# Column norms summed over partitions on GpSimd instead of by fp32 matmuls, and the library that this needs

## The chip, the cores and the metric

One core of a Trainium2 chip. The time is that of one whole execution in device microseconds (us). It differs from run to run by some tenths of a per cent, so medians of several runs are given. Kernels are compared with runs of the kernel before on the same chip. A ratio is the mean time of one kernel's fast runs over that of the other's fast runs of the same rounds, so it is not quite the ratio of the medians quoted beside it. A profile's span is some 1.8 us shorter than the time of its run.

PE is TensorE, ACT is ScalarE, DVE is VectorE and POOL is GpSimd. GpSimd also issues all loads of q, k, v and the weights.

## The reference, cut to what matters

```python
def _attn_ref(q, k, v, tau):                  # q, k, v: 4 x 5824 x 256, fp32
    qn = q / (np.linalg.norm(q, axis=1, keepdims=True) + 1e-06)
    kn = k / (np.linalg.norm(k, axis=1, keepdims=True) + 1e-06)
    s = kn.transpose(0, 2, 1) @ qn / tau      # 256 x 256 for each batch
    ...                                       # softmax of s over its last axis -> a
    return (v @ a).astype(np.float32)

def _moe_ref(x, w1, w2, w3, w_out):           # x: the result above, 23296 x 256
    a = x @ w1
    b = x @ w2
    h = a * b @ w3
    return (h @ w_out).astype(np.float32)
```

The norms run over the 5824 tokens. Tokens lie on partitions, so a norm needs a sum over partitions.

## The kernel before

The softmax matrix of a batch is folded into w1 and w2 ("Wf"), and w3 into w_out. The bulk of the work is then two wide products a and b for each chunk of v, their product on DVE, and one product o. While batch b goes through this, the scores of batch b+1 are accumulated (G), and the squares of its q and k are summed over time into one 128 x 2 x 256 tile. After the last score come the steps that I call the **tail** of batch b: sum over partitions, inverse norms, scaling, exponentials, row sums, folding. The steps are placed by a list of times on a clock of the kernel's own, near microseconds:

```python
def norms():
    a1 = work.tile([P, 2, C], F32, tag="acc1", ...)
    nc.vector.tensor_add(a1, accs[n][:, 0], accs[n][:, 1])
    st["ksq"] = a1[:, 1, :]
    st["qsq"] = a1[:, 0, :]
def k_row():
    m = psum.tile([P, 512], F32, tag="ab", ...)
    nc.tensor.matmul(m[:, :C], lhsT=ones_pp, rhs=st["ksq"], start=True, stop=True)   # fp32
    ...   # four activations: Ln, Exp, Ln, Exp
def q_sums():
    m = psum.tile([P, 512], F32, tag="ab", ...)
    for ct in range(CT):
        nc.tensor.matmul(m[:, ct:ct + 1], lhsT=st["qsq"][...], rhs=ones_f, ...)      # fp32
    q_norm(m[:, :CT])   # two activations, two small DVE instructions
...
# in the list of times: norms, k_row, q_sums, scaled (scaling and exponentials), sums, eight folds
ts = [t1 + 1.0, t1 + 3.5, t1 + 4.0, t1 + 8.0, t1 + 12.0] + [t1 + 13.0 + 0.9 * i for i in range(8)]
```

At the start GpSimd issues loads and, after the first two pieces, builds an identity matrix:

```python
load_piece("k", 0, 0, (half,))
load_piece("q", 0, 0, (half,))
masks.make_identity(nc, ident)      # on GpSimd: a memset and an affine select
nc.vector.tensor_copy(ident_b, ident)
...
for pi in range(1, 4):
    load_piece("k", 0, pi)
    load_piece("q", 0, pi)
```

## Time and profile before

| what | before |
|---|---|
| median of 4 runs | 575.73 us (575.41 to 576.57) |
| span of the profile; PE busy in it | 573.6; 561.9 us |
| mean granted PE clock | 1.000 |
| fp32 matmuls in one tail, from PE's starts | 0.80 us |

To see where time goes I cut the span at the first 'a' matmul of each batch. PE's timeline of the kernel before (start, length, engine, line, operation, count):

```profile
40.15 0.59 PE L425 MATMUL a<-vT,Wf 128*128 128x512 bf16 x2
...
183.03 0.59 PE L425 MATMUL a<-vT,Wf 128*128 128x512 bf16 x2
...
316.73 0.59 PE L425 MATMUL a<-vT,Wf 128*128 128x512 bf16 x2
...
450.10 0.59 PE L425 MATMUL a<-vT,Wf 128*128 128x512 bf16 x2
```

The differences are the stretches: start 40.15, batch 0 142.88, batch 1 133.70, batch 2 133.37 and batch 3 123.50 us. A tail lies in each of batches 0, 1 and 2.

### The profile page before, as it was taken

To read this page: it belongs to the slowest core of one execution; us is meant where nothing else is said; L and a number is where in the kernel's file an instruction comes from. 1 tells how busy PE (TensorE), PEld (TensorE's weight loads), DVE (VectorE), ACT (ScalarE), POOL (GpSimd) and SP (SyncE) were. 2 spreads that over 40 slices of the span, in tenths; PEclk is the share of its full clock that TensorE was granted. 3 is DMA by queue.
4 is the path that set the end of the run, shared out by engine and by line. 5 is a ranking of instruction groups with operands and counts; after the bars stand their busy time and mean duration, and the time that the engine had idled before them with its cause. 6 is when DMAs were issued, how large, how long until landed. Compare 5 with 4: busy or idle time off the path is not lost.

```text
span 573.6 us, 10125 instructions
## 1 busy us (share of the span) xinstructions
PE 561.9 (98%) x3760; PEld 357.0 (62%) x3766; DVE 374.1 (65%) x597; ACT 337.9 (59%) x624; POOL 71.0 (12%) x162
## 2 busy tenths in 40 slices
PE   8789999999999999999999999999999999999997
PEld 4755576776666666666666666666665666666665
DVE  0047744787967567887776567778876656565564
ACT  0046534777766567776765567767765555454453
POOL 5240020202010111221000012021100000000000
PEclk9999999999999999999999999999999999999999
DMA  8999959779574696495661596675740325221011
GB/s 163 211 194 208 188 99 235 175 171 213 134 185 108 123 207 151 95 190 120 147 147 49 117 192 143 132 142 119 184 110 38 85 74 146 63 63 74 38 71 59
DMA packets 74561, 76.93 MB, mean 134 GB/s; under 512 B 54161, under 2 KB 58257, under 8 KB 74513
## 3 DMA queue, kind: packets, MB, share of 16 engines
q0 software_dynamic: 15504, 39.46, 39.2%
q1 hardware_dynamic: 58784, 36.64, 21.1%
q8 instruction: 29, 0.48, 0.3%
q10 hardware_dynamic: 224, 0.20, 0.1%
q14 instruction: 20, 0.16, 0.1%
HBM read 78.91 MB, written 23.86 MB: 179 GB/s over the span
## 4 chain that ended last, share of the span: by engine, by line
PE 91%; DMA 5%; ACT 1%; issue 1%; DVE 1%; POOL 1%; ACTq 0%; POOLq 0%
PE o L466 27%; PE a L425 27%; PE b L425 27%; PE G L188 5%; DMA k<-in_k_dram 3%; PE fold L344 2%; DMA q<-in_q_dram 2%; PE w L575 1%; ACT as L431 1%; POOL k L109 0%; PE row L272 0%; POOL q L109 0%; DVE abs L440 0%; DVE osb L487 0%; ACT kr L276 0%
## 5 line engine op out<-in xcount | busy, mean ns | idle before, releaser
L440 DVE TENSOR_TENSOR abs<-as,b 128x512 bf16<-128x512 bf16 x336 | 229.7, 685 | 140.5 <-ACT as L431 128.7
L431 ACT CAST as<-a 128x512 bf16<-128x512 f32 (+1 forms) x384 | 215.4, 562 | 177.7 <-PE a L425 86.7
L425 PEld LDWEIGHTS <-Wf 128*128 128x128 bf16 x1536 | 149.1, 98 | 102.5 <-issue 2.6
L466 PE MATMUL o<-W_sb,abs 128*128 128x256 bf16 x1376 | 209.7, 273 | 0.5 <-ACT osb L486 0.4
L425 PE MATMUL a<-vT,Wf 128*128 128x512 bf16 x704 | 209.4, 379 | 0.4
L425 PE MATMUL b<-vT,Wf 128*128 128x512 bf16 x704 | 209.4, 379 | 0.0
L466 PEld LDWEIGHTS <-abs 128*128 128x128 bf16 x1376 | 134.5, 98 | 82.0 <-issue 0.6
L197 DVE TENSOR_TENSOR acc<-acc,sq 128x1024 f32<-128x1024 f32 x66 | 80.4, 1219 | 0.8 <-ACT sq L185 0.8
L188 PE MATMUL G<-k,q 128*128 128x256 bf16 x276 | 49.6, 273 | 0.0
L185 ACT ACTIVATE sq<-q 128x512 f32<-128x512 bf16 x66 | 41.8, 633 | 0.0
L185 ACT ACTIVATE sq<-k 128x512 f32<-128x512 bf16 x66 | 41.6, 630 | 0.0
L413 POOL COPY gate_t<-abs 1x1 bf16<-1x1 bf16 x39 | 12.1, 310 | 183.7 <-DVE abs L440 183.1
L487 DVE COPY osb<-o 128x512 f32<-128x512 f32 x44 | 30.1, 684 | 0.0
L188 PEld LDWEIGHTS <-q 128*128 128x128 bf16 x276 | 27.0, 98 | 3.1
L486 ACT COPY osb<-o 128x512 f32<-128x512 f32 x44 | 25.7, 585 | 4.6 <-PE o L466 2.6
L417 POOL COPY gate_t<-vT 1x1 bf16<-1x1 bf16 x17 | 4.0, 234 | 180.5 <-DMA vT<-v 145.1
L274 ACT ACTIVATE kr<-row 128x256 f32<-128x256 f32 x4 | 1.5, 384 | 34.0 <-PE row L272 34.0
L109 POOL DMA_DIRECT2D q<-in_q_dram x29 | 15.6, 538 | 12.5 <-DMA k<-in_k_dram 5.2
L344 PE MATMUL fold<-w,e 128*128 128x512 bf16 x61 | 16.5, 378 | 0.1
L351 ACT ACTIVATE Wf<-fold,rs 128x512 bf16<-128x512 f32 x16 | 10.9, 687 | 7.2 <-PE fold L344 4.3
L109 POOL DMA_DIRECT2D k<-in_k_dram x25 | 13.7, 550 | 3.9 <-DMA k<-in_k_dram 1.9
L109 POOL DMA_DIRECT2D v<-in_v_dram x25 | 13.4, 539 | 4.0 <-issue 2.6
(87 smaller groups left out, 219.1 us busy)
## 6 DMA issues: line engine op xcount, KB each, us to landing
out_dram<-osb SPq DMA_DIRECT2D x44, 512.0 KB, 3.1
k<-in_k_dram POOLq DMA_DIRECT2D x19, 512.0 KB, 8.8
v<-in_v_dram POOLq DMA_DIRECT2D x19, 512.0 KB, 5.1
q<-in_q_dram POOLq DMA_DIRECT2D x18, 512.0 KB, 6.5
w_wout<-in_moe_w_dram POOLq DMA_DIRECT2D x1, 2048.0 KB, 22.9
k<-in_k_dram POOLq DMA_DIRECT2D x4, 320.0 KB, 9.4
v<-in_v_dram POOLq DMA_DIRECT2D x4, 320.0 KB, 5.2
q<-in_q_dram POOLq DMA_DIRECT2D x4, 256.0 KB, 11.9
```

Source lines behind the costliest of these rows:

```text
L109: nc.gpsimd.dma_start(out=pieces[nm, n, pi][:, lo:hi, :], in_=qk_main[nm, n][0][:, pi * PIECE + lo : pi * PIECE + hi, :])
L185: nc.scalar.activation(out=dst[:, :, part, :], in_=src[:, o : o + 2, :], func=AF.Square)
L188: nc.tensor.matmul(G[:, ct, :], lhsT=qt[:, i, ct * P : (ct + 1) * P], rhs=kt[:, i, :], start=(pr == 0 and part == 0 and ct == 0), stop=(pr ...
L197: nc.vector.tensor_add(accs[n], accs[n], sqs[0])
L344: nc.tensor.matmul(st["fold", i], lhsT=st["e"][:, c2, c1 * P : (c1 + 1) * P], rhs=w12[:, c2, w, h * 512 : (h + 1) * 512], start=(c2 == 0), ...
L413: nc.gpsimd.tensor_copy(gate_t, last_ab[0][:1, :1])
L425: nc.tensor.matmul(t[:, :n], lhsT=Wf[b][:, ct, w, j * P : (j + 1) * P], rhs=rhs_of(b, c, ct), start=(ct == 0), stop=(ct == CT - 1),)
L431: nc.scalar.copy(a_sb[:, :n], tiles[0][:, :n])
L440: nc.vector.tensor_mul(ab, a_sb, tiles[1])
L466: nc.tensor.matmul(tl[h][:, o, :], lhsT=lhsT, rhs=W_sb[:, j, :], start=(j == 0 and o == 0), stop=(j == FT - 1 and (small or o == 1)), skip ...
L486: nc.scalar.copy(o[:, 0:2, :], tl[0])
L487: nc.vector.tensor_copy(o[:, 2:4, :], tl[1])
```

## The change

Its intent: take the fp32 matmuls from PE, the bound engine, and let idle GpSimd sum over partitions. The identity moves behind six pieces' load issues, so that a library load that GpSimd needs stands there. The tail's steps get new times, to leave room for the reduction. Cut to its core:

```diff
         def norms():
             nc.vector.tensor_add(a1, accs[n][:, 0], accs[n][:, 1])
-            st["ksq"] = a1[:, 1, :]
-            st["qsq"] = a1[:, 0, :]
+            tot = work.tile([P, 2, C], F32, tag="s", name=f"tot_{n}", bufs=1)
+            nc.gpsimd.partition_all_reduce(
+                tot.rearrange("p w c -> p (w c)"), a1.rearrange("p w c -> p (w c)"), P, ReduceOp.add
+            )
+            st["tot"] = tot
 ...  # k_row: the four activations read tot, no matmul, where n > 0
         def q_sums():
-            ...  # two fp32 matmuls
-            q_norm(m[:, :CT])
+            q_norm(diagonal(st["tot"][:, 0, :].rearrange("p (c t) -> p c t", t=P)))
 ...
-    masks.make_identity(nc, ident)
-    nc.vector.tensor_copy(ident_b, ident)
 ...
     for pi in range(1, 4):
+        if pi == 3:
+
+            masks.make_identity(nc, ident)
+            nc.vector.tensor_copy(ident_b, ident)
         load_piece("k", 0, pi)
 ...
-            t0, t1 = 58.0, 120.0
+            t0, t1 = 58.0, 118.0
 ...
-        ts = [t1 + 1.0, t1 + 3.5, t1 + 4.0, t1 + 8.0, t1 + 12.0] + [t1 + 13.0 + 0.9 * i for i in range(8)]
+        ts = [t1 + 1.0, t1 + 8.5, t1 + 9.0, t1 + 11.0, t1 + 14.5] + [t1 + 15.5 + 0.9 * i for i in range(8)]
```

"diagonal" multiplies two 128x128 blocks by the identity on DVE and sums each row, as batch 0 does before too.

## The prediction

> **What bounds the kernel now.** I read the page's busy table first, then the stretches of the span, then the three places where the removed matmuls stand, then the start. The busy table:
>
> ```profile
> PE 561.9 (98%) x3760; PEld 357.0 (62%) x3766; DVE 374.1 (65%) x597; ACT 337.9 (59%) x624; POOL 71.0 (12%) x162
> ```
>
> TensorE (PE) is busy for 561.9 of 573.6 us at full granted clock, so 11.7 us is all its idle time. GpSimd (POOL) has 88% of the span free. Taking matmuls from PE therefore shortens the span by about what they occupied, if nothing else makes PE wait. Their place in the first batch's tail, in PE's timeline (start, length, operation, count):
>
> ```profile
> 163.52 0.60 PE L466 MATMUL o<-W_sb,abs 128*128 128x256 bf16 x4
> 163.95 0.60 PE L272 MATMUL row<-acc,ones_pp 128*128 128x256 f32 x2
> 164.39 0.50 PE L283 MATMUL ss<-ones_f,acc 128*128 128x1 f32 x4
> 164.75 0.59 PE L425 MATMUL a<-vT,Wf 128*128 128x512 bf16 x2
> ...
> 167.71 0.38 PE L466 MATMUL o<-W_sb,abs 128*128 128x256 bf16 x2 [0.39 <-ACT osb L486]
> ```
>
> Lengths overlap because matmuls are pipelined; the cost is the distance between starts. The two fp32 groups hold PE from 163.95 to 164.75: 0.80 us. In the two later tails the same distance is 291.22 to 292.01 and 425.14 to 425.94, so 0.79 and 0.80 us. The last line is PE waiting 0.39 us for ScalarE (ACT), which the same norms had occupied:
>
> ```profile
> 163.29 0.58 ACT L431 CAST as<-a 128x512 bf16<-128x512 f32 x1 [0.71 <-PE a L425]
> 164.59 0.38 ACT L274 ACTIVATE kr<-row 128x256 f32<-128x256 f32 x1 [0.72 <-PE row L272]
> ...
> 166.50 0.21 ACT L292 ACTIVATE r<-r 128x2 f32<-128x2 f32 x1
> 166.61 0.56 ACT L431 CAST as<-a 128x512 bf16<-128x512 f32 x1
> ```
>
> Six activations hold ACT from 164.59 to 166.61, about 2.0 us, while every group of matmuls (1.30 us) leaves ACT only 0.7 us idle.
>
> The start is another regime: PE waits for loads. In the stretches (length, busy time by engine, clock, DMA share, GB/s) the transfers are saturated from 5 us on:
>
> ```profile
> 0.00:5.00 5.00, 3.75 (x9) 1.34 (x10) 0.91 (x7) 1.28 (x1) 3.89 (x12) 1.00 0.50 69
> 5.00:10.00 5.00, 5.00 (x40) 3.03 (x39) 0.00 (x0) 0.00 (x0) 3.28 (x7) 1.00 1.12 215
> 10.00:15.00 5.00, 4.06 (x55) 3.44 (x54) 0.17 (x1) 0.00 (x0) 1.05 (x2) 1.00 1.05 211
> 15.00:20.00 5.00, 2.97 (x36) 2.52 (x34) 0.00 (x0) 0.00 (x0) 0.56 (x1) 1.00 1.06 213
> ```
>
> GpSimd issues those loads. Its timeline shows that after eight issues (six pieces, the first two in halves) each further one waits until an earlier load has landed:
>
> ```profile
> 3.78 0.29 POOL masks.py:199 TENSOR_SCALAR_AFFINE_SELECT ident<-ident 128x128 f32<-128x128 f32 x1
> ...
> 5.60 0.57 POOL L109 DMA_DIRECT2D q<-in_q_dram  x1
> ...
> 8.06 0.53 POOL L109 DMA_DIRECT2D k<-in_k_dram  x1 [0.72 <-DMA q<-in_q_dram]
> 9.37 0.53 POOL L109 DMA_DIRECT2D q<-in_q_dram  x1 [0.78 <-DMA q<-in_q_dram]
> ```
>
> **What the Trainium skill says.** (1) "FP8 and Floating Point Precision", section TensorE Precision Notes: true fp32 is "4 passes through PE array". The trace agrees: the fp32 row of 256 columns holds PE for 0.44 us from start to start, as long as the four bf16 matmuls of 256 columns ahead of it (163.52 to 163.95, 0.43 us). (2) "GPSIMD Engine Reference", section 2.1: the first call to a freshly loaded kernel pays a load of approximately 6 us that shows as no instruction. The trace before can't show this: the identity's select begins within 0.1 us of the memset before it. (3) The same page, section 3: a two-input GpSimd operation runs at about 2.6 cycles an element at 1.2 GHz, and a partition-axis tensor_reduce of [128, 2048] takes 247,699 ns. No run here shows either. (4) "SBUF - State Buffer", section Who interferes with whom: a VectorE (DVE) instruction with at most one SBUF input outside the two-port modes doesn't contend with GpSimd. The tail's products read one operand from PSUM and last 0.69 us; I expect them unchanged beside the reduction.
>
> **The change part by part.**
>
> Removed: the row and the column sums of three tails. 0.80 + 0.79 + 0.80 = 2.39 us of PE on the path that sets the end. This is the certain gain: **-2.4 us**.
>
> Added on GpSimd: one all-reduce of 128x512 fp32 per tail. My estimate takes the page's 2.6 cycles: one pass over 512 elements is 512 x 2.6 / 1.2 GHz = 1.1 us, and folding partitions, passing sums along the cores and writing back is three to five such passes, so 3.3 to 5.5 us. In the tail after batch 0 the sum that feeds it is ready at 163.1 (DVE's 0.68 us from 162.40), and the schedule now puts the consumers 7.5 us of its own clock after the reduction, where it was 2.5. So it should be done before ACT asks. It also stays clear of the transfers: GpSimd issues one load at 161.11 and the next work is at 169.94. In the other tails it may delay the next issue by some 3 us, for a batch that starts some 20 us later. Cost on the path: 0.
>
> Added on DVE: per tail two custom reductions against the identity. Batch 0 already does this, at 288 ns each plus 82 ns for reading the accumulator: 2 x 370 = 0.74 us. DVE idles 2.15 us in that place now, waiting for ACT's r. Cost: 0, or a tenth.
>
> Moved on ACT: the six activations stay, 2.0 us. Before, PE spent 0.80 us on fp32 work meanwhile; now the next a and b matmuls follow at once. ACT can start the row in the 0.7 us gap, so its backlog is 2.0 + 0.1 - 0.7 = 1.4 us, where before the next copy was late by 166.61 - (164.75 + 0.71) = 1.15 us. Further, the exponentials come 2.5 units after the row instead of 4.5, so the backlog has drained less (0.7 us a group, so two groups) when 0.91 us of exponentials arrive. Four PSUM buffers of a and b give about 1 us of slack: copy and product end some 2.05 us after a's start, and the b matmul that takes the buffer again starts 3.03 us after it. The excess is 0.2 to 0.4 us a tail; I charge 0.2 a tail: **+0.6 us**.
>
> Moved at the start: the identity, with the library load in front of its select, now stands behind six pieces. Those issues end near 5.5 us. Six pieces are 3.15 MB; with 0.35 MB moved by 5 us (69 GB/s x 5) and then 213 GB/s, they last until 5 + 2.80/0.213 = 18.2 us. A first transfer took about 2 us to flow (issue at 1.23, 0.35 MB at 210 GB/s before 5.0 means a start near 3.3), and engines end unevenly (the sixth piece is waited for until 19.95), so the next issue must come by about 14 us. With a load of 6 us it comes at 5.5 + 6 + 0.6 = 12.1: hidden. With 10 us it comes at 16: up to 2 us lost. Weighing both: **+0.4 us**. The identity itself isn't needed before 32 us.
>
> Sum: -2.4 + 0.6 + 0.4 = -1.4 us, so 575.8 - 1.4 = **574.4 us**.
>
> **The rivals.**
>
> (A) ACT becomes the wait. For it: the 0.39 us stall above; the row, column norm and exponentials are packed closer. Against: ACT is 59% busy, and PE loses only about 0.65 us in the whole of the first tail and 0.18 us in each of the others. If every tail lost 1 us more, the gain is gone: about 576.5 to 577.
>
> (B) The library load starves the start. For it: the only regime where PE waits for transfers, and a load under saturated DMA may be slower than the page's 6 us. At 15 us the next issue comes at 21, some 5 to 7 us late, which goes to the end one for one: 579 to 581.
>
> (C) The reduction is much slower than thought. The page's 247.7 us for 2048 columns would be some 62 us for 512, and three such waits on ACT would make 700 us or more. Against: it is another instruction, and a schedule that leaves 7.5 us was hardly set for 62. At 10 us, ACT would hold up some 3 us a tail, and the time would be near 582.
>
> (D) All is hidden and the stall of 0.39 us goes too: 573.0, the floor of a pure removal.
>
> **Range and chances.** The pure removal gives 573.4, with the stall gone 573.0; three runs before spread over 1.2 us, so the low end is 572.2. Upwards, A with a late library load gives 577 to 578. So 572.2 to 578.0. Two per cent is 11.5 us: the removal cannot give it, with 2.4 us of PE touched, and only C or an extreme B could take it. Faster 0.01, same 0.97, slower 0.02.
>
> **What would show it right or wrong.** PE: 18 fp32 matmul records fewer, busy time down by 2 to 2.4 us. GpSimd: three reductions of 3 to 6 us, each ended before the first activation of the row reads it. ACT: the row's first activation waits for nothing or for the previous copy; if GpSimd is named as releaser, C holds in part. PE's waits in the tails: under 0.5 us each for ACT; over 1 us means A. Start: a hole on GpSimd after 5.5 us before the identity's select; the first 'a' matmul of batch 0 (40.15 before) within 1 us of where it was, later under B. A DMA rate under 200 GB/s between 15 and 20 us would show starvation. I am wrong if the library load stands in a tail instead of the start, or if that first 'a' matmul moves by over 2 us.

## The result, and the profile after

The changed kernel took **583.65 us** (581.52 to 584.32, 4 runs) against 575.73: ratio 1.0129, 95% interval 1.0101 to 1.0157. That is slower, within two per cent, and outside the range that I gave. The same cuts in PE's timeline of the changed kernel:

```profile
42.27 0.59 PE L430 MATMUL a<-vT,Wf 128*128 128x512 bf16 x2
...
191.04 0.60 PE L430 MATMUL a<-vT,Wf 128*128 128x512 bf16 x2
...
324.82 0.59 PE L430 MATMUL a<-vT,Wf 128*128 128x512 bf16 x2
...
458.54 0.59 PE L430 MATMUL a<-vT,Wf 128*128 128x512 bf16 x2
```

| stretch | before | after | difference |
|---|---|---|---|
| start | 40.15 | 42.27 | +2.12 |
| batch 0 | 142.88 | 148.77 | +5.89 |
| batch 1 | 133.70 | 133.78 | +0.08 |
| batch 2 | 133.37 | 133.72 | +0.35 |
| batch 3 | 123.50 | 123.56 | +0.06 |
| span | 573.6 | 582.1 | +8.50 |

PE's busy time rose from 561.9 to 563.2 us, though 18 fp32 matmul records are gone. Part of its matmuls ran at a lower clock.

**The start.** GpSimd's timeline of the changed kernel (a bracket tells the idle time before, and what ended it):

```profile
5.52 0.28 POOL masks.py:197 MEMSET ident<- 128x128 f32 x1
18.62 0.28 POOL masks.py:199 TENSOR_SCALAR_AFFINE_SELECT ident<-ident 128x128 f32<-128x128 f32 x1 [12.82 <-issue]
18.88 0.74 POOL L110 DMA_DIRECT2D k<-in_k_dram  x1
```

Between memset and select lie 12.8 us in which GpSimd does nothing that the profile counts, and the next load issue waits behind it. The transfers run short in the stretches (length, busy time by engine, clock, DMA share, GB/s):

```profile
10.00:15.00 5.00, 2.19 (x24) 1.42 (x23) 0.00 (x0) 0.00 (x0) 0.00 (x0) 1.00 1.06 205
15.00:20.00 5.00, 4.89 (x43) 4.24 (x44) 0.53 (x3) 0.00 (x0) 1.36 (x3) 0.66 0.74 147
20.00:25.00 5.00, 4.19 (x55) 3.57 (x54) 0.00 (x0) 0.00 (x0) 3.85 (x8) 1.00 0.98 174
```

147 and 174 GB/s stand where the kernel before had 213 and 215. The shortfall is (66 + 41) GB/s x 5 us = 0.54 MB, or 2.5 us at 213 GB/s, near the 2.12 us that the start is longer. This is a working and not a test: the second line also shows PE at a clock of 0.66 (third figure from the right), which may have its part.

**The first tail.** GpSimd, ACT and PE in the changed kernel:

```profile
163.17 0.53 POOL L110 DMA_DIRECT2D v<-in_v_dram  x1 [0.34 <-issue]
170.91 3.25 POOL L258 PARTITION_ALL_REDUCE tot<-acc  x1 [7.21 <-DVE abs L445]
...
174.19 0.42 ACT L272 ACTIVATE kr<-tot 128x256 f32<-128x256 f32 x1 [4.30 <-POOL tot L258]
...
172.13 0.60 PE L471 MATMUL o<-W_sb,abs 128*128 128x256 bf16 x4
176.89 1.01 PE L430 MATMUL a<-vT,Wf 128*128 128x512 bf16 x2 [4.16 <-ACT as L436]
177.70 1.06 PE L430 MATMUL b<-vT,Wf 128*128 128x512 bf16 x2
```

The reduction's input was complete at 163.57 (DVE's sum, 0.68 us from 162.89). It started at 170.91, after 7.2 us of GpSimd idle time. The releaser named, a product on DVE, is only inferred by the profile; in the runs with one library and with the early second load the reduction starts at 163.34 and 163.95 beside the same products, so they are not the cause. ACT waits 4.30 us for the reduction and does no copies meanwhile. PE waits 4.16 us for a copy. After that gap PE runs at about half speed: 'a' to 'b' takes 0.81 us from start to start instead of 0.43. The stretch from 172 to 184 us, first of the kernel before, then of the changed one, shows the granted clock at 1.00 and 0.72 (the same figure):

```profile
172.00:184.00 12.00, 11.73 (x86) 7.53 (x86) 8.91 (x27) 7.19 (x17) 0.00 (x0) 1.00 0.58 130
```

```profile
172.00:184.00 12.00, 7.79 (x41) 4.49 (x41) 4.92 (x16) 5.58 (x14) 3.74 (x5) 0.72 0.54 107
```

From the starts: the gap costs 176.89 - 172.13 - 0.44 = 4.3 us, and two groups of 2.5 us instead of 1.3 and one short one cost 2.7 us more. Less the 0.8 us of fp32 matmuls and the 0.4 us wait that tail had before, this makes 5.8 us, as measured (5.89).

**The later tails.** Their reductions start at once, take 3.24 us and keep nobody waiting. But PE waits again, as in the third tail (first ACT's exponentials, then PE):

```profile
443.18 0.91 ACT L312 ACTIVATE e<-s,r 128x256 bf16<-128x256 f32 x2 [1.31 <-DVE s L307]
...
443.19 0.60 PE L471 MATMUL o<-W_sb,abs 128*128 128x256 bf16 x4
444.61 0.24 PE L328 MATMUL sum<-ones_b,e 128*128 128x1 bf16 x4 [0.82 <-ACT as L436]
445.10 0.59 PE L430 MATMUL a<-vT,Wf 128*128 128x512 bf16 x2 [0.25 <-ACT as L436]
```

That is 1.07 us for ACT, which eats the 0.80 us saved. ACT does no copies for 1.31 us of idle time, until DVE has scaled the scores, and then for 0.91 us of exponentials. The kernel before has the same idle time (1.09 us at 296.96), but there the copies had caught up first: one that began at 295.28 had waited for PE.

So three causes are to be tested: the 12.8 us hole, the 7.2 us hole, and the waits for ACT. The order of instructions on GpSimd gives a lead. A library load has no record in the trace, but it stands in the program, as an "ISA" row without operands:

```
13 masks.py:199 ISA
14 masks.py:199 TensorScalarAffineSelect ident<-ident 128x128
...
75 L110 DMACopy v_2_2007<-in_v_dram 128x2048
76 L258 ISA
77 L258 ISA tot_2043<-acc_1_2041 128x512
```

There are two loads, not one: library 0 ahead of the identity's select, and library 1 ahead of the first reduction. The kernel before has the first of them too, and there the select starts within 0.1 us of the memset.

**Theory T**, of residency: a load costs time only if another library is resident. The changed kernel ends each execution with library 1, so the next one must load library 0 at its start and library 1 again in its first tail. **Rival R**: the load costs its 12.8 us at that place whatever is resident. **Rival D**: the first reduction is late for another reason than a load. For the later tails, **theory S**: the spacing of the tail's steps crowds ACT. **Rival P**: the reduction itself costs PE that time.

### The profile page after: what moved, and what is told of

Its sections match the earlier page's. It is cut to its first block, busy times and chain, and to the rows that moved or that the text cites. A ratio compares the mean times of both kernels' runs of the same rounds, so it can differ in the third digit from the quotient of the medians.

```text
span 582.1 us, 10090 instructions
## 1 busy us (share of the span) xinstructions
PE 563.2 (97%) x3742; PEld 356.4 (61%) x3748; DVE 376.9 (65%) x609; ACT 337.3 (58%) x624; POOL 83.9 (14%) x165
## 4 chain that ended last, share of the span: by engine, by line
PE 87%; ACT 4%; issue 3%; DVE 2%; DMA 2%; POOL 2%; POOLq 0%; ACTq 0%; DVEq 0%
PE a L430 26%; PE o L471 26%; PE b L430 26%; PE G L189 5%; PE fold L349 2%; DMA k<-in_k_dram 2%; ACT as L436 2%; DVE abs L445 1%; PE w L582 1%; POOL k L110 1%; POOL q L110 1%; POOL tot L258 1%; ACT e L312 0%; ACT kr L274 0%; ACT kr L273 0%
## 5 line engine op out<-in xcount | busy, mean ns | idle before, releaser
L418 POOL COPY gate_t<-abs 1x1 bf16<-1x1 bf16 x39 | 14.6, 375 | 173.0 <-DVE abs L445 172.2
```

Of the source, the lines that this page charges most:

```text
L418: nc.gpsimd.tensor_copy(gate_t, last_ab[0][:1, :1])
```

## The experiments

The first four ran on one chip, against 575.71 us of the kernel before.

**One library.** Library 1 carries both the select and the reduction; loading it by name ahead of the identity leaves that one load in the program.

```diff
+            nc.gpsimd.load_library(library_config._reserved_1)
             masks.make_identity(nc, ident)
```

> The changed kernel with one explicit load of the library that carries both the identity's select and the reduction, ahead of the identity; nothing else differs. Theory T (residency: a load costs time only if another library is resident; the changed kernel switches to the select's library at its start and back in the first tail, and ends each execution with the second one): after the first execution nothing needs loading, no hole on GpSimd before the select, first 'a' matmul of batch 0 near 40.2 us, first reduction near 163.6 us within 0.5 us of its data, no throttled clock, total 575 to 577 us. Rival R (any load ahead of the select costs its 12.8 us, whichever library is resident): the hole of 12 to 13 us stays, first 'a' near 42.3, total 577.5 to 579. Rival D (the first reduction is late for another reason than a load, such as sharing a port with VectorE): reduction still 7 us late, total above 581.

Measured: 576.15 us (575.93 to 577.51), ratio 1.0009 (0.9992 to 1.0026). GpSimd in this run:

```profile
5.72 0.28 POOL masks.py:197 MEMSET ident<- 128x128 f32 x1
6.08 0.29 POOL masks.py:199 TENSOR_SCALAR_AFFINE_SELECT ident<-ident 128x128 f32<-128x128 f32 x1
...
163.34 3.18 POOL L259 PARTITION_ALL_REDUCE tot<-acc  x1
```

Both holes are gone, and the first 'a' matmul is at 40.22. R and D fall. The profiled execution was the slowest of the four (577.51), with a 1.4 us wait for a load of k in batch 0; its waits in the later tails are as in the changed kernel.

**The identity moved, nothing else.** To the kernel before:

```diff
-    masks.make_identity(nc, ident)
-    nc.vector.tensor_copy(ident_b, ident)
 ...
     for pi in range(1, 4):
+        if pi == 3:
+            masks.make_identity(nc, ident)
+            nc.vector.tensor_copy(ident_b, ident)
```

> The kernel before, with the identity and its copy moved behind six pieces as in the change, and nothing else. Theory T: the select's library is resident from the execution before, so no hole: total within 0.5 us of the kernel before (575.3 to 576.3). Rival (the new place itself starves the transfers): first 'a' matmul 1 to 2 us later, 577 to 578.

Measured: 575.29 us (575.17 to 575.66), ratio 0.9997 (0.9982 to 1.0011). The select begins 0.1 us after its memset has ended, and the first 'a' is at 40.09. The place is harmless.

**Two loads without a reduction.** To the run above, in the tail of batch 0 alone:

```diff
         def norms():
+            if n == 1:
+                nc.gpsimd.load_library(library_config._reserved_1)
```

> The run above plus a load of the reduction's library in the first tail, where the change has it, but no reduction: norms stay on fp32 matmuls. Theory T: this load makes the next execution load the select's library at its start, so a hole of 12 to 13 us on GpSimd before the select and the first 'a' matmul 2 us later, though nothing at the start was edited; the load in the tail delays only GpSimd. Total 577.3 to 578.5. Rival R (the hole belongs to the changed start or to the reduction): no hole, total 575.3 to 576.3.

Measured: 578.39 us (576.85 to 579.35), ratio 1.0047 (1.0027 to 1.0066). GpSimd's start:

```profile
5.53 0.28 POOL masks.py:197 MEMSET ident<- 128x128 f32 x1
16.94 0.28 POOL masks.py:199 TENSOR_SCALAR_AFFINE_SELECT ident<-ident 128x128 f32<-128x128 f32 x1 [11.13 <-issue]
```

An edit at about 165 us of the program opened a hole of 11.1 us at its start (12 to 13 were expected). The start is that of the run above, which has no hole, and there is no reduction: what the first load costs depends on the rest of the program. That the library left by the execution before decides it, as T says, is inferred: a load that is skipped because the whole program needs no other library would give the same runs, and no run tells the two apart. In this profile the first 'a' came at 43.89, 3.74 us late instead of the 2 expected, but it was one of the two slower runs of four, and PE's clock was 0.78 and 0.87 in the stretches from 25 to 30 and 30 to 35 us. The tail itself lost nothing: batch 0 took 142.87 us.

**The second load earlier.** To the changed kernel:

```diff
             t0, t1 = 58.0, 118.0
+            at(111.0, 0.0, lambda: nc.gpsimd.load_library(library_config._reserved_1))
```

> The changed kernel with its second load asked for about 8 us of schedule earlier, behind the issue of an earlier load of v, where GpSimd is idle. Theory T: the hole at the start stays (first 'a' near 42.3 us), the first reduction starts within 0.5 us of its data (near 163.6), ScalarE does not wait for it, PE's clock stays at 1.00 in that tail, and batch 0 from its first to its last 'a' matmul takes 143 us instead of 148.8: total 577.3 to 578.3. Rival D: reduction late again, total above 581.

Measured: 577.80 us (577.49 to 579.13), ratio 1.0044 (1.0029 to 1.0059). The hole at the start is 12.4 us and the first 'a' at 42.30; the reduction starts at 163.95, and the clock in the tail is back:

```profile
162.00:186.00 24.00, 22.81 (x153) 13.79 (x152) 16.79 (x45) 14.56 (x34) 5.73 (x8) 1.00 0.63 148
```

Batch 0 takes 142.87 us instead of 148.77. The place of the second load alone is worth 5.9 us, including the throttled clock.

That leaves the waits for ACT. With one library the kernel stands 0.4 us above the kernel before, with 2.4 us of matmuls removed. The next three shared another chip, with the kernel before at 575.59 us; the last two were set against 575.59 as well.

**Spacing restored, row moved ahead.** To the run with one library:

```diff
-        ts = [t1 + 1.0, t1 + 8.5, t1 + 9.0, t1 + 11.0, t1 + 14.5] + [t1 + 15.5 + 0.9 * i for i in range(8)]
+        ts = [t1 + 1.0, t1 + 5.5, t1 + 6.0, t1 + 10.0, t1 + 14.0] + [t1 + 15.0 + 0.9 * i for i in range(8)]
```

> The run with one library, with the norms' steps in the tails spaced as in the kernel before: row 4.5 units after the reduction instead of 7.5, scaling 4.5 after the row instead of 2.5, sums 4 after the scaling instead of 3.5. Theory S (the 2.4 us that the fp32 matmuls gave up are lost again because row, scaling, exponentials and sums now follow each other too closely on ScalarE, about 1.1 us of PE wait a tail): these waits fall under 0.3 us a tail, batches 1 and 2 take 132.9 and 132.6 us from first 'a' to first 'a' matmul instead of 133.8 and 133.7, total 573.0 to 574.0. Rival P (the waits come from the reduction itself, its port or its result in SBUF): waits stay at about 1 us a tail, total 575.5 to 576.5.

Measured: 579.44 us (578.96 to 583.28), ratio 1.0077 (1.0057 to 1.0097). Neither expectation held. ACT's and PE's lines of the second tail say why:

```profile
295.37 0.42 ACT L273 ACTIVATE kr<-tot 128x256 f32<-128x256 f32 x1 [1.38 <-POOL gate_t L423]
...
297.75 0.59 PE L431 MATMUL a<-vT,Wf 128*128 128x512 bf16 x2 [0.91 <-ACT as L437]
```

The reduction ran from 292.11 to 295.34, and ACT reached the row 1.38 us too early (the releaser named is the instruction after it on GpSimd). So my edit put the reduction itself on the path, and the run does not tell S from P. It does show that the row's 7.5 units behind the reduction in the change are needed in part.

**The kernel before, crowded.** Fp32 matmuls kept, the change's spacing:

```diff
-        ts = [t1 + 1.0, t1 + 3.5, t1 + 4.0, t1 + 8.0, t1 + 12.0] + [t1 + 13.0 + 0.9 * i for i in range(8)]
+        ts = [t1 + 1.0, t1 + 3.5, t1 + 4.0, t1 + 6.0, t1 + 9.5] + [t1 + 10.5 + 0.9 * i for i in range(8)]
```

> The kernel before with its fp32 matmuls, no reduction and no library, but with the change's spacing: scaling 2.0 units after the column sums, sums 3.5 after the scaling. Theory S: PE waits for ScalarE by 0.5 to 1.1 us a tail, total 577 to 579. Rival P: no new waits, total 575.3 to 576.2.

Measured: 577.58 us (577.21 to 578.71), ratio 1.0040 (1.0025 to 1.0054). Each of the three batches with a tail became 0.65 to 0.67 us longer, with a new wait in the second tail:

```profile
297.58 0.59 PE L425 MATMUL a<-vT,Wf 128*128 128x512 bf16 x2 [0.71 <-ACT as L431]
```

There is no reduction here, so spacing alone makes such waits. That is for S.

**The row cut into pairs.** As the run with restored spacing, with the six activations in three pairs, each at a time of its own:

```diff
+        def k_row_2():   # the row's second Ln and Exp
 ...
-        head = [(0.0, norms), (0.0, k_row), (0.0, q_sums)]
+        head = [(0.0, norms), (0.0, k_row), (0.0, k_row_2), (0.0, q_sums)]
 ...
+        ts = [t1 + 1.0, t1 + 5.5, t1 + 7.2, t1 + 8.9, t1 + 11.0, t1 + 15.0] + [t1 + 16.0 + 0.9 * i for i in range(8)]
```

> As the run with restored spacing, with the six activations of the norms cut into three pairs, one for each group of matmuls, so that each fits ScalarE's idle gap of 0.7 us. Theory S: the last waits of PE for ScalarE in the tails go too, total 572.6 to 573.6, by 0 to 0.5 us faster than without the cut, and 2 to 3 us faster than the kernel before. Rival P: no gain, 575.5 to 576.5.

Measured: 576.09 us (575.70 to 576.39), ratio 1.0008 (0.9996 to 1.0020): a miss for S, and inside the range that was named for P. ACT still waits 1.38 us for the reduction. Later an output copy (0.60 us from 300.13) is followed by 1.31 us in which ACT waits for DVE's scaling, and by the exponentials, with no copy of 'a' in between. PE's wait follows at 303.46:

```profile
302.04 0.91 ACT L318 ACTIVATE e<-s,r 128x256 bf16<-128x256 f32 x2 [1.31 <-DVE s L313]
...
303.46 0.59 PE L436 MATMUL a<-vT,Wf 128*128 128x512 bf16 x2 [0.67 <-ACT as L442]
```

My guess from this was that the exponentials must also keep clear of the output copies, some 11 us apart here (289.23 and 300.13), and the row of the reduction's end. The last two runs do both at once, so the output copy's own part is not shown.

**Scaling later.** To the run with one library:

```diff
-        ts = [t1 + 1.0, t1 + 8.5, t1 + 9.0, t1 + 11.0, t1 + 14.5] + [t1 + 15.5 + 0.9 * i for i in range(8)]
+        ts = [t1 + 1.0, t1 + 8.5, t1 + 9.0, t1 + 13.5, t1 + 17.0] + [t1 + 18.0 + 0.8 * i for i in range(8)]
```

The folds also follow each other at 0.8 units instead of 0.9, which the expectation does not mention.

> The run with one library, with one edit: scaling, sums and folds of the tails come 2.5 units later (scaling 5 units after the row instead of 2.5, so also clear of the output copies that come every 10.4 us), the row where it was, so that it does not wait for the reduction as it did in the two runs whose row was moved ahead. Theory S: PE's waits for ScalarE in the tails fall from 1.07 us to under 0.4 us each; batches 1 and 2 take 132.8 to 133.1 us from first 'a' to first 'a'; total 573.2 to 574.4. Rival P (the reduction on GpSimd itself costs PE about 1 us a tail): waits stay, 575.7 to 576.5.

Measured: **573.69 us** (573.67 to 573.86), ratio 0.9968 (0.9953 to 0.9982). PE's waits for ACT (total, times, longest), first with one library and the change's spacing, then here:

```profile
PE sum L329 <- ACT as L437: 1.6, 2, 0.8
...
PE a L431 <- ACT as L437: 1.2, 3, 0.7
```

```profile
PE a L431 <- ACT as L437: 0.5, 2, 0.3
```

Batches 1 and 2 take 132.68 and 132.88 us instead of 133.78 and 133.72. The reduction is the same (3.19 to 3.23 us), so P falls.

**Pairs, all later.** As the run with pairs, at these times:

```diff
+        ts = [t1 + 1.0, t1 + 7.0, t1 + 8.3, t1 + 9.6, t1 + 13.2, t1 + 16.8] + [t1 + 17.8 + 0.8 * i for i in range(8)]
```

> The same idea with the six activations cut into three pairs (one a group of matmuls), the first pair at 7.0 units, after the reduction's end, scaling at 13.2. Theory S: no wait of PE for ScalarE over 0.3 us in tails two and three, total 572.8 to 574.0, within 0.4 us of the run without the cut. Rival P: 575.7 to 576.5.

Measured: 573.76 us (573.54 to 573.79), ratio 0.9967 (0.9952 to 0.9981). Cutting the row adds nothing once the steps are apart.

The version with one library and later scaling beats both kernels: 1.9 us (0.3%) under the kernel before, and 10 us under the changed one as it ran on its own chip. By the two per cent measure it is the same as the kernel before.

## Why the prediction was wrong, point by point

The terms of its sum, beside what they came to. Crowding is the stretch's difference plus the 0.80 us removed, for batch 0 from the run with the early second load (142.87 - 142.88 + 0.80). It is thus a remainder, and the first row is what the fp32 matmuls occupied in the kernel before:

| step of the prediction | charged | measured |
|---|---|---|
| Removed: fp32 matmuls | -2.4 | -2.4 |
| Added on GpSimd, first tail | 0 | +5.9 |
| Moved on ACT (crowding) | +0.6 | 0.8 + 0.9 + 1.15 = +2.8 |
| Moved at the start | +0.4 | +2.1 |
| batch 3 | 0 | +0.1 |
| sum | -1.4 | +8.5 |

**The step that failed** is "Added on GpSimd ... So it should be done before ACT asks. ... Cost on the path: 0". I took the reduction as starting when its input was ready, and one library load as standing in front of the select. The program has a second load in front of the first reduction. It made that reduction 7.2 us late, ACT waited 4.3 us for it, and PE lost 4.3 us in a gap and then 2.7 us while its clock was lower; moving that load alone gave 5.9 us back. The prediction's last sentence names a load in a tail as what would make it wrong, but gives it no time and no chance; and it did not think of loads in both places. The clock was in no rival.

**Moved at the start** had the right mechanism and a wrong size. The prediction took 6 us from the page and weighed it against 10; the hole was 12.8 us. Rival B, "the library load starves the start", is what happened, with the signs that the prediction named: under 200 GB/s from 15 to 20 us (147) and the first 'a' over 2 us late (2.12). It was weaker than drawn: with a next issue due by 14 us and made at 18.9, the prediction's own sum gives 4.9 us, and 2.1 were lost. The reason for the load was not seen: the kernel before has the same load instruction and pays nothing.

**Moved on ACT** was right in mechanism, as rival A says; the term was 0.6 and measured 2.8 us. The prediction charged 0.2 us a tail where 0.8 to 1.15 were lost. Later scaling won back 0.45, 1.10 and 0.84 us of these (142.87 to 142.42, 133.78 to 132.68, 133.72 to 132.88), so 2.4 of the 2.8 us go with the times of the steps. The prediction counted 0.91 us of exponentials against the slack. It left out the 1.31 us in which ACT waits for DVE's scaling ahead of them (1.09 us at 296.96 in the trace before, where it could have been read) and the output copy; which of the two weighs more is not shown.

**Right**: the removal on PE, of which 1.9 of 2.4 us became time once the libraries and the spacing were mended; the duration, 3.24 us against 3.3 to 5.5; DVE's products undisturbed (687 ns against 685 in the groups by line); no harm to loads in the tails. Rival C, a reduction of 10 us or more, did not happen, but a late reduction acts on ACT in the way C describes.

**Open**: why one load takes 12.8 us at the start and 7.2 in the tail. The DMA share was 1.06 (10 to 15 us) and 0.71 (162 to 172 us), which fits a load that shares the transfers, but no run varied that alone. Nor is it shown what sets the clock down after PE's gap; only that without the gap it stays at 1.00. At the start the clock was 0.66 between 15 and 20 us; with the early second load, where the hole (12.4 us) and the first 'a' (42.30) are nearly the same, it was 1.00 there and 0.66 between 25 and 30. How much of the 2.1 us is the clock's and how much the transfers', no run separates. And whether a load is skipped because of what the last execution left, or because of what the program needs as a whole, stays open.

## What to carry to other kernels

Before moving work to GpSimd, list which library each of its instructions needs and choose one that carries them all: the kernels with two libraries paid for the load at the start (11.1 to 12.8 us of GpSimd's time) and, where something waited for it, for the second (7.2 us) as well. ACT's wait of 4.3 us held up the copies behind it, and the gap of some 4 us that this left on PE was followed by another 2.7 us lost at a lower clock. When a step leaves the bound engine, spread what follows it on the other engines again, or the gain is lost in small waits.

## What the Trainium skill lacked or had wrong

- "GPSIMD Engine Reference", section 2.1, gives approximately 6 us for the first call to a freshly loaded kernel. The runs show 7.2 us in the middle of the kernel and 11.1 to 12.8 us at its start, with transfers saturated. That no instruction shows in the profile agrees.
- No page that I read says when a library load costs nothing (under 0.1 us in the kernel before), nor that a second library in a program makes the first load cost time too. The run with two loads and no reduction shows it: a hole of 11.1 us at a start that is the same as in the run above it, where the select begins within 0.1 us. That the resident library outlives an execution would explain it, and is not shown.
- "GPSIMD Engine Reference", section 3.2, gives 247,699 ns for a tensor_reduce along partitions at [128, 2048], and no figure for the all-reduce over partitions. That one takes 3.24 us at 128x512 fp32 here; a quarter of the page's figure would be 62 us, so it must not be scaled to this instruction.
